# The order of two weight loads at the seam of a scan-and-routing kernel, and the place of four sums

## Chip, cores and metric

One core of a Trainium2 chip. The metric is the device time of one execution in microseconds (us). The kernel before was run three times; one further execution was profiled. PE is TensorE (PEld its weight loads), DVE is VectorE, ACT is ScalarE, POOL is GpSimd, and SP is the queue of SyncE, from which most DMAs are issued.

## What is computed

An attention block (a chunked state-space scan) gives one row of 256 numbers for each of 3072 tokens. Then each token goes through one of eight experts, chosen by its id; the order of the tokens is that of the batch and the sequence.

```python
# scan, per chunk c of 32 steps (batch 4, 8 heads, 768 steps, head dim 32, state dim 16)
y_intra = einsum('bhij,bhjd->bhid', CB * L, xc)
y_inter = einsum('bhin,bhnd->bhid', Cc, state) * decay_to_i
state   = decay_full * state + sum_j(B_j x_j decay_from_j)
# bridge: (B,H,S,D) -> (B*S, H*D) = (3072, 256)
expert_idx = token_ids * 2654435761 % 8
for e in range(8):
    xe = x[expert_idx == e]
    out[expert_idx == e] = maximum(xe @ w1[e], 0) @ w2[e]     # 256 -> 1024 -> 256
```

## The kernel before, in words

**Two parts.** The scan runs first, in six pairs of 64 steps; its rows y are stored to the DRAM tensor `y_tokens` (L407). A routing table is computed meanwhile. The second part goes over the experts in an order of falling token counts; the p-th expert in that order is called place p (`regs[p]` holds its number). Its tokens are taken from `y_tokens` by indirect DMAs on POOL (`gather`, L628, one tile of 128 tokens each), transposed on PE (`turn`, L636, or `early`, L648) and copied out of PSUM into `xT` (by DVE at L654, by ACT at L642).

**Seven products for eight.** Each product of an expert is cut in two by two blocks and done as seven block products with sums of operands in the manner of Strassen and Winograd. `sums_w(p, 1, j, eng)` (L782) makes the four weight sums of place p's first weights, from `w` into `s`; `sums_w(p, 2, j, eng)` those of the second weights; `sums_x` (L882) the four sums of a place's tokens, in `t1`; `sums_h` (L891 to L898) those of its hidden rows, in `t2`. The sums of one set are used in the order 2, 1, 3, 0 of their slices. `up(p, q0, what)` (L917) does block product `what` for two of the four row blocks of the hidden layer; 1 and 2 need weights as loaded, of the first half only, and the early token slots; 3, 5, 6 and 7 need the weight sums, 4 the second half of the weights. The products 6, 7 and 4 add onto one PSUM bank, which DVE reads in between (u2, L932; u3, L935; hx, L941), and 5 and 3 onto another (L944, L939). `down(p, what)` (L964) does the same for the second product.

**Loads.** `load_w1(p, i)` (L616) loads half i of place p's first weights, 512 KB; `load_w2(p)` (L620) the second weights, 1024 KB. All are issued by SP, in program order: an instruction of SP that waits holds up all behind it.

**The seam.** The token slots are laid out so that the first halves of places 0 to 3 (tiles 0 to 6, called EK) come from the first 16 of 24 blocks of steps and can be gathered early. Place 3's early slots are 600 to 792, tiles 4, 5 and 6. Tiles 7 and 8 (`need(0)`) hold place 0's second half; they are gathered when the last store of y has landed. A loop over `seq`, m = 0 to 15, does products 1 and 2 of places 0 to 3 on the early slots. Into it are put: the transposes of tiles 2 to 6 (m = 2, 6, 10), DVE's weight sums of places 0, 1 and 2 (m = 5, 8 and 11), the transposes of the two late tiles (m = 13, 14) and DVE's token sums of place 0 (m = 15). m = 12 to 15 are place 3's products. Right behind m = 0, SP gets a DMA of one number from the last late tile into `held` (L1051), which makes SP wait until that tile has landed, and then three loads.

**The steps.** `step(p)` does, interleaved over its rounds r, the remaining up-products of place p and the down-products of place p - 1, the transposes and gathers of later places, POOL's weight sums (`sums_w(p, 2, ...)` and, from step 1 on, `sums_w(p + 2, 1, ...)`) and DVE's token and hidden sums. Step 0 has five rounds, with the up-products 6, 7, 5, 4, 3. The order of each engine's instructions is the order of the program.

```python
    for w in ((1, 1), (2, 1), (3, 0)):                       # L1025
        load_w1(*w)
...
        if m == 8:                                           # L1038
            for j in range(4):
                sums_w(1, 1, j, dve)
        if m == 11:
            for j in range(4):
                sums_w(2, 1, j, dve)
...
        if m == 0:                                           # L1050
            sp_e.dma_start(out=held[:], in_=xg[need(0)[-1]][0:1, 0:1])
            for w in (0, (3, 1), 1):
                load_w2(w) if isinstance(w, int) else load_w1(*w)
```

Of the kernel before, what the change touches and what calls it, by code (L numbers as in the profile page):

```python
# [25 lines left out]
def kernel(  # L26
# [12 lines left out]
    dve, act, pe, pool_e, sp_e = nc.vector, nc.scalar, nc.tensor, nc.gpsimd, nc.sync  # L39
# [7 lines left out]
    E, _, F = moe_w1.shape  # L47
# [564 lines left out]
    def load_w1(p, i, eng=sp_e):  # L612
        if p not in w1s:
            w1s[p] = (w4[0] if p % 4 == 3 else wpool).tile([P, DP, F], F32, name="w1")
        src = moe_w1[bass.ds(regs[p], 1), :, i * FH:(i + 1) * FH].rearrange("e (k p) f -> p (e k) f", p=P)
        eng.dma_start(out=w1s[p][:, :, i * FH:(i + 1) * FH], in_=src)  # L616

    def load_w2(p, eng=sp_e):
        w2s[p] = wx[0].tile([P, FP, DM], F32, name="w2", bufs=2)
        eng.dma_start(out=w2s[p], in_=moe_w2[bass.ds(regs[p], 1)].rearrange("e (k p) d -> p (e k) d", p=P))  # L620
# [139 lines left out]
    def early(m):  # L760
        turn_pair([q for q in EK if q // 2 == m], (3, 2, 7, 6)[m], dve)
# [3 lines left out]
    def sums_w(p, layer, i, eng):  # L765

        if layer == 1:
            w = w1s[p]
            q = lambda i, k: w[:, k, i * FH:(i + 1) * FH]
            if p not in s1:  # L770
                s1[p] = (spool if p % 3 else s1pool).tile([P, 4, FH], F32, name="s1")
            s = s1[p]
        else:
            w = w2s[p]
            q = lambda i, k: w[:, k * Q4:(k + 1) * Q4, i * P:(i + 1) * P]
            if p not in s2:
                s2[p] = spool.tile([P, 4, Q4, P], F32, name="s2")
            s = s2[p]
        i = (2, 1, 3, 0)[i]
        a_, b_, o = ((q(1, 0), q(1, 1), OP.add), (s[:, 2], q(1, 1), OP.add), (q(1, 0), q(0, 0), OP.subtract),  # L780
                     (q(0, 1), s[:, 1], OP.subtract))[i]
        eng.tensor_tensor(out=s[:, i], in0=a_, in1=b_, op=o)  # L782
        if eng is pool_e and i in (0, 3):
            eng.tensor_copy(out=space, in_=s[:, i, 0, 0:1] if layer == 2 else s[:, i, 0:1])
# [90 lines left out]
    def sums_x(p, i):  # L875
        n = HALF[p]
        q = lambda k, j: xT[:, k, slots(p, j)]
        if i == 0:
            t1[p] = mwork.tile([P, 4, N0], F32, name="t1")
        t = t1[p][:, :, 0:n]  # L880
        a_, b_ = ((q(0, 1), q(0, 0)), (q(1, 1), t[:, 0]), (q(0, 1), q(1, 1)), (q(1, 0), t[:, 1]))[i]
        dve.tensor_tensor(out=t[:, i], in0=a_, in1=b_, op=OP.subtract)  # L882

    def sums_h(p, i):
        n = HALF[p]
        if i == 0:
            t2[p] = hpool.tile([P, 4, Q4, N0], F32, name="t2", bufs=1)
        t = t2[p][:, :, :, 0:n]
        q = lambda k, j: hx[p][:, {(0, 1): 0, (1, 0): 1, (1, 1): 2}[k, j], :, 0:n]
        if i == 0:  # L890
            dve.scalar_tensor_tensor(out=t[:, 0], in0=q(0, 1), scalar=0.0, in1=h11[p][:, :, 0:n],  # L891
                                     op0=OP.max, op1=OP.subtract)
        elif i == 1:
            dve.tensor_tensor(out=t[:, 1], in0=q(1, 1), in1=t[:, 0], op=OP.subtract)
        elif i == 2:
            dve.scalar_tensor_tensor(out=t[:, 2], in0=q(0, 1), scalar=0.0, in1=q(1, 1), op0=OP.max, op1=OP.subtract)  # L896
        else:
            dve.tensor_tensor(out=t[:, 3], in0=q(1, 0), in1=t[:, 1], op=OP.subtract)  # L898
# [100 lines left out]
    def scatter(o_sb, idx):  # L999
        st = pool_e.indirect_dma_start(  # L1000
            out=out[:], out_offset=bass.IndirectOffsetOnAxis(ap=idx, axis=0),
            in_=o_sb, in_offset=None, bounds_check=NT - 1, oob_is_err=False)
        tc.declare_no_dep(st.ins, group="out_rows", reason="distinct rows")
        tc.add_to_no_dep_group("out_rows", st.ins)
# [12 lines left out]
    def turn(k):  # L1017
        if k not in turned:
            turn_x(k, XB)
            turned.add(k)  # L1020
# [1 line left out]
    need = lambda p: [k for k in tiles_of(p) if k not in EK] if p < E else []  # L1022
    outs = sorted(range(NK), key=lambda k: (done_at[k], k))

    for w in ((1, 1), (2, 1), (3, 0)):  # L1025
        load_w1(*w)
    ask(need(0))
    first = [(p, q0) for p in range(NEAR) for q0 in (0, 2)]
# [3 lines left out]
    for m, (what, i) in enumerate(seq):  # L1032
        if m in (2, 6, 10):
            early((m + 2) // 4)
        if m == 5:
            for j in range(2, 4):
                sums_w(0, 1, j, dve)
        if m == 8:  # L1038
            for j in range(4):
                sums_w(1, 1, j, dve)  # L1040
        if m == 11:
            for j in range(4):
                sums_w(2, 1, j, dve)
        if m in (13, 14):
            turn(need(0)[m - 13])
        if m == 15:
            for j in range(4):
                sums_x(0, j)
        up(*first[i], what, banks=(i % 6,) * 2)
        if m == 0:  # L1050
            sp_e.dma_start(out=held[:], in_=xg[need(0)[-1]][0:1, 0:1])  # L1051
            for w in (0, (3, 1), 1):
                load_w2(w) if isinstance(w, int) else load_w1(*w)

    UP = [1, 6, 2, 7, 5, 4, 3]
    UP_E = [6, 7, 5, 4, 3]
    DOWN = [1, 2, 6, 5, 7, 4, 3]

    def step(p):

        ups = [] if p == E else UP_E if p < NEAR else UP
        downs = DOWN if p > 0 else []
        turns = [k for k in need(p + 1) if k not in turned]
        puts = [k for k in outs if done_at[k] == p - 2]
        gets = [k for w in ((2,), (3, 4))[p] for k in need(w) if k not in asked] if p < 2 else need(p + 3)
        sums = [(p, 2, i) for i in range(4)] if p < E else []
        sums += [(p + 2, 1, i) for i in range(4)] if 0 < p < E - 2 else []
        xs_ = [(p + 1, i) for i in range(4)] if p + 1 < E else []
        R = 5 if p == 0 else 7
        off = 0 if p == 0 else (R - len(ups)) // 2  # L1070
        sent = []
        for r in range(R):
            if p > 0 and (r == 0 or p >= NEAR and r < 4):
                sums_h(p - 1, r)
            if sent:
                scatter(*sent.pop(0))
            if gets and p == 0:
                ask(gets)
                gets = []
            if 0 <= r - off < len(ups):  # L1080
                up(p, 0, ups[r - off])
            if turns:
                turn(turns.pop(0))
            if puts:
                sent.append(put(puts.pop(0)))
            if sums and not (p == 1 and r < 4):
                sums_w(*sums.pop(0), pool_e)
            if gets and r >= 1:
                ask([gets.pop(0)])
            if 0 <= r - off < len(ups):  # L1090
                up(p, 2, ups[r - off])
            if 0 < p < NEAR and 0 < r < 4:
                sums_h(p - 1, r)
            if sums and r == 3 and p != 1:
                sums_w(*sums.pop(0), pool_e)
            if p >= NEAR and r >= 3 and not turns and xs_:
                sums_x(*xs_.pop(0))
            if p == 1 and r == 4:
                pool_e.tensor_copy(out=space, in_=t2[0][:, 3, 0, 0:1])
            if p == E - 1 and r == R - 1:  # L1100
                sums_h(p, 0)
            if downs:
                down(p - 1, downs[r])
                if downs[r] == 4 and p + 1 < E:
                    load_w2(p + 1)
            if p < NEAR and r >= (2 if p == 0 else 3) and not turns and xs_:
                sums_x(*xs_.pop(0))
        while xs_ or turns:
            if turns:
                turn(turns.pop(0))  # L1110
            else:
                sums_x(*xs_.pop(0))
        for o in sent:
            scatter(*o)
        for v in sums:
            sums_w(*v, pool_e)
        if p + 4 < E:
            load_w1(p + 4, 0)
            load_w1(p + 4, 1)
        for k in gets:  # L1120
            ask([k])

    for p in range(E):
        step(p)
# [48 lines left out]
    for m in range(2):  # L1173
        scatter(o_own[m], idx_out[:, rest[m]:rest[m] + 1])

    _, rn = nc.values_load_multi_w_load_instructions(
        nov_i[0:1, 0:1], min_val=0, max_val=NCH + E,
        skip_runtime_bounds_check_because="a count of tiles: at most one an expert besides the full ones")
    kf = route.tile([P, 1], F32)
    dve.memset(kf, float(NK))  # L1180
    with tc.For_i(0, rn[0], 1):
# [9 lines left out]
        for c in range(NCH):  # L1191
# [14 lines left out]
        _, re = nc.values_load_multi_w_load_instructions(  # L1206
            ei_i[0:1, 0:1], engines=[ET.SP], min_val=0, max_val=E - 1,
            skip_runtime_bounds_check_because="an expert's number, clamped to E - 1")
# [52 lines left out]
```

## Time and profile before

| | |
|---|---|
| three runs | 231.1, 235.72, 237.67 us (median 235.72) |
| the profiled execution | 231.41 us, its span 229.7 us |
| PE busy | 213.5 us, 93% of the span |
| DVE busy | 180.7 us, 79% |
| POOL busy | 172.4 us, 75% |
| ACT busy | 89.4 us, 39% |
| mean granted TensorE clock | 0.992 of full speed |

A busy share is an average over stages with different limits. Matmuls are pipelined, so that a busy PE is an engine with work in it. Times in rows count from the first instruction of the execution. In a row of the timeline the bracket at the end gives the idle time of that engine just before the instruction, and what ended it.

### The profile page before, as it was taken

What the parts mean: (1) busy time and instruction counts of PE and PEld (TensorE: products, weight loads), DVE (VectorE), ACT (ScalarE), POOL (GpSimd) and SP (SyncE); (2) the same over time, 40 slices, a digit from 0 to 9 for tenths busy, and PEclk for the clock granted to TensorE, in tenths of its full rate; (3) what the DMA queues carried; (4) which work ended last, traced back from release to release, by engine and by line L of the source; (5) the groups of instructions that cost most, each with busy time, mean ns of one, the idle gap of its engine ahead of it and who ended that gap; (6) DMA issues with size and microseconds to landing.
All of it is one profiled execution on the core that took longest, in us unless ns stands there. A gap on an engine that the chain in (4) does not pass through costs nothing.

```text
span 229.7 us, 5853 instructions
## 1 busy us (share of the span) xinstructions
PE 213.5 (93%) x2266; PEld 200.5 (87%) x2266; DVE 180.7 (79%) x314; ACT 89.4 (39%) x190; POOL 172.4 (75%) x220
## 2 busy tenths in 40 slices
PE   6889989998786899999999999999999999999990
PEld 2778878877685799999999999999999999999980
DVE  7868899798547688899997998697489979956630
ACT  4774965954443551312123214234323411413210
POOL 7977367866717198489988998999799999996342
PEclk9999999999999999999999999999999999999996
DMA  6999799999888885029019119307005112401011
GB/s 136 162 200 127 181 191 177 174 185 302 273 218 259 253 267 199 24 75 332 30 62 334 64 47 339 118 7 244 26 24 204 33 45 79 175 23 47 24 70 43
DMA packets 49877, 33.16 MB, mean 144 GB/s; under 512 B 26632, under 2 KB 44184, under 8 KB 49850
## 3 DMA queue, kind: packets, MB, share of 16 engines
q1 hardware_dynamic: 46786, 25.76, 45.6%
q0 software_dynamic: 2400, 6.43, 8.5%
q10 hardware_dynamic: 664, 0.61, 1.1%
q8 instruction: 18, 0.29, 0.5%
q14 instruction: 9, 0.07, 0.1%
HBM read 26.49 MB, written 6.42 MB: 143 GB/s over the span
## 4 chain that ended last, share of the span: by engine, by line
PE 73%; DMA 8%; DVE 7%; ACT 6%; issue 2%; SPq 1%; POOL 1%; ACTq 0%; DVEq 0%; POOLq 0%
PE ps L964 31%; PE ps L917 28%; PE ps L315 4%; DMA w<-in_moe_w_dram 3%; DMA xg<-y_tokens,idx_in 3%; PE ps L991 2%; PE ps L374 2%; PE ps L636 2%; DMA y_tokens<-y_sb 2%; DVE m L321 1%; ACT z L358 1%; PE ps L387 1%; PE ps L269 1%; DVE rows L259 1%; ACT ct L289 1%
## 5 line engine op out<-in xcount | busy, mean ns | idle before, releaser
L628 POOL DMA_INDIRECT xg<-y_tokens,idx_in x25 | 30.2, 1206 | 17.1 <-issue 10.1
L917 PE MATMUL ps<-t,s 128*128 128x202 f32 (+7 forms) x192 | 37.1, 328 | 0.6 <-DVE t L882 0.6
L782 POOL TENSOR_TENSOR s<-w 128x512 f32<-128x512 f32 x26 | 33.2, 1277 | 5.7 <-DMA w<-in_moe_w_dram 5.5
L1000 POOL DMA_INDIRECT out_dram<-o_sb,idx_out x25 | 26.4, 1056 | 12.5 <-ACT o_sb L996 6.7
L964 PE MATMUL ps<-t,s 128*128 128x202 f32 (+7 forms) x192 | 35.5, 326 | 0.0
L917 PEld LDWEIGHTS ps<-t,s 128*128 128x128 f32 x192 | 31.5, 190 | 1.3 <-ACT h L927 0.9
L964 PEld LDWEIGHTS ps<-t,s 128*128 128x128 f32 x192 | 31.8, 189 | 0.3 <-issue 0.3
L917 PE MATMUL ps<-xT,w 128*128 128x200 f32 (+7 forms) x128 | 24.9, 329 | 3.0 <-DMA w<-in_moe_w_dram 2.3
L917 PEld LDWEIGHTS ps<-xT,w 128*128 128x128 f32 x128 | 20.7, 190 | 3.8 <-DVE s L782 2.5
L945 ACT ACTIVATE hx<-hx 128x404 f32<-128x404 f32 (+7 forms) x16 | 8.3, 525 | 31.8 <-DVE hx L944 31.3
L321 DVE COPY_PREDICATED m<-cmask,ps 128x1024 f32<-128x1024 int32 x12 | 15.5, 1320 | 3.6 <-PE ps L315 3.6
L782 POOL TENSOR_TENSOR s<-w,s 128x512 f32<-128x512 f32 x13 | 17.6, 1351 | 0.5
L782 POOL TENSOR_TENSOR s<-s,w 128x512 f32<-128x512 f32 x13 | 17.3, 1327 | 0.5
L882 DVE TENSOR_TENSOR t<-xT 128x202 f32<-128x202 f32 (+7 forms) x16 | 16.4, 1024 | 0.8 <-ACT xT L642 0.8
L923 ACT ACTIVATE p<-ps 128x404 f32<-128x404 f32 (+7 forms) x16 | 7.9, 492 | 20.0 <-PE ps L917 19.7
L374 PEld LDWEIGHTS ps<-x_t,m 128*64 128x64 f32 x384 | 12.1, 138 | 3.0 <-issue 1.3
L374 PE MATMUL ps<-x_t,m 128*64 128x64 f32 x384 | 13.4, 224 | 1.1 <-ACT y_sb L401 0.6
L315 PE MATMUL ps<-ce,bt 32*64 32x128 f32 x384 | 12.9, 274 | 1.1 <-ACT ce L289 0.7
L882 DVE TENSOR_TENSOR t<-xT,t 128x202 f32<-128x202 f32 (+7 forms) x16 | 13.7, 854 | 0.0
L896 DVE SCALAR_TENSOR_TENSOR t<-hx 128x808 f32<-128x808 f32 (+7 forms) x8 | 13.3, 1660 | 0.0
L315 PEld LDWEIGHTS ps<-ce,bt 32*64 32x64 f32 x384 | 10.4, 132 | 2.5 <-ACT ce L289 0.9
L358 ACT ACTIVATE z<-z,half 128x256 f32<-128x256 f32 x22 | 10.0, 504 | 6.6 <-DVE z L352 6.6
(201 smaller groups left out, 472.5 us busy)
## 6 DMA issues: line engine op xcount, KB each, us to landing
w<-in_moe_w_dram SPq DMA_DIRECT2D x16, 512.0 KB, 7.1
w<-in_moe_w_dram SPq DMA_DIRECT2D x8, 1024.0 KB, 8.0
x_t<-in_x_dram SPq DMA_DIRECT2D x12, 256.0 KB, 6.2
y_tokens<-y_sb SPq DMA_DIRECT2D x10, 256.0 KB, 4.3
raw<-in_B_dram SPq DMA_DIRECT2D x12, 128.0 KB, 3.5
raw<-in_C_dram SPq DMA_DIRECT2D x12, 128.0 KB, 3.5
y_tokens<-y_sb ACTq DMA_DIRECT2D x2, 256.0 KB
xg<-y_tokens,idx_in POOLq DMA_INDIRECT x25, 3.5
```

What stands on the lines that cost most here:

```text
L315: pe.matmul(out=ps[u * T:(u + 1) * T, GB + g, b * P:(b + 1) * P].rearrange("q (e i) -> q e i", e=2), lhsT=bts[ck][r, b, c], rhs=ces[ck][r, ...
L321: dve.copy_predicated(out=m_sb[k % 2][:, g0:g1].rearrange("q g b i -> q g (b i)"), mask=cmask.bitcast(I32).rearrange("q j i -> q (j i)").u ...
L358: act.activation(z4s[un][:, :, j], zs[un].rearrange("q b e d -> q b (e d)"), AF.Copy, scale=half4[:, j:j + 1])
L374: pe.matmul(out=o, lhsT=m_sb[k % 2][:, g, b, e * T:(e + 1) * T], rhs=xs[k][:, b, 2 * g + e], start=first(g // 2 * 2 + b % 2, c), stop=True ...
L628: pool_e.indirect_dma_start(out=xg[k], out_offset=None, in_=y_dram[0:n, :], in_offset=bass.IndirectOffsetOnAxis(ap=idx_in[:, k:k + 1], axi ...
L782: eng.tensor_tensor(out=s[:, i], in0=a_, in1=b_, op=o)
L882: dve.tensor_tensor(out=t[:, i], in0=a_, in1=b_, op=OP.subtract)
L896: dve.scalar_tensor_tensor(out=t[:, 2], in0=q(0, 1), scalar=0.0, in1=q(1, 1), op0=OP.max, op1=OP.subtract)
L917: pe.matmul(out=ps[:, bank, i * n:(i + 1) * n], lhsT=lhs[:, (q0 + i) * P:(q0 + i + 1) * P], rhs=rhs, start=(first and i == 0), stop=True, ...
L945: act.activation(hq(2), hq(2), AF.Relu)
L964: pe.matmul(out=ps[:, bank, 0:n], lhsT=lhs(q), rhs=rhs(q), start=(first and q == 0), stop=True, skip_group_check=True)
L1000: st = pool_e.indirect_dma_start(out=out[:], out_offset=bass.IndirectOffsetOnAxis(ap=idx, axis=0), in_=o_sb, in_offset=None, bounds_check= ...
```

## The change

Of the three loads ahead of the seam's loop, (2,1) is taken out and put first behind the `held` DMA. The loads ahead of the loop are now (1,1), (3,0); behind `held` come (2,1), the second weights of place 0, (3,1), and the second weights of place 1. The four DVE sums of place 2's first weights leave m = 11 and go into step 0, one in each of the rounds 0 to 3, behind the round's second up-product.

```diff
-    for w in ((1, 1), (2, 1), (3, 0)):
+    for w in ((1, 1), (3, 0)):
         load_w1(*w)
...
-        if m == 11:
-            for j in range(4):
-                sums_w(2, 1, j, dve)
...
         if m == 0:
             sp_e.dma_start(out=held[:], in_=xg[need(0)[-1]][0:1, 0:1])
-            for w in (0, (3, 1), 1):
+            for w in ((2, 1), 0, (3, 1), 1):
                 load_w2(w) if isinstance(w, int) else load_w1(*w)
 
+    late_sums = [0, 1, 2, 3]
...
             if p == E - 1 and r == R - 1:
                 sums_h(p, 0)
+            if p == 0:
+                for _ in range((1, 1, 1, 1, 0)[r]):
+                    sums_w(2, 1, late_sums.pop(0), dve)
             if downs:
                 down(p - 1, downs[r])
```

## Rows read from the trace of the kernel before

**Rows 1.** The page's first line: the span and its instructions.
```profile
span 229.7 us, 5853 instructions
```
**Rows 2.** Busy by stretch: length, PE, PEld, DVE, ACT, POOL (instructions); clock; DMA; GB/s.
```profile
72.00:74.00 2.00, 0.18 (x1) 0.21 (x2) 1.97 (x5) 0.09 (x1) 1.39 (x3) 1.00 0.62 217
78.00:214.00 136.00, 136.00 (x854) 134.84 (x855) 114.63 (x173) 39.82 (x97) 115.29 (x111) 1.00 0.37 125
```
**Rows 3.** Timeline of PE, seam to step 1: start, duration, line, operation, tiles, count.
```profile
73.82 0.89 PE L917 MATMUL ps<-xT,w 128*128 128x192 f32 x4 [2.27 <-DMA w<-in_moe_w_dram]
...
77.89 0.95 PE L917 MATMUL ps<-t,s 128*128 128x202 f32 x4 [0.58 <-DVE t L882]
...
86.96 1.51 PE L917 MATMUL ps<-t,s 128*128 128x200 f32 x8
...
89.69 1.52 PE L917 MATMUL ps<-t,s 128*128 128x200 f32 x8
91.04 1.53 PE L964 MATMUL ps<-t,s 128*128 128x202 f32 x8
```
**Rows 4.** From the chain that ended last, 44 to 92 us: load (3,0), issue to landing.
```profile
66.55 7.14 DMA w<-in_moe_w_dram
```
**Rows 5.** Timeline of the SP queue at the seam: issues of weight loads and `held`.
```profile
64.82 2.10 SPq L616 DMA_DIRECT2D w<-in_moe_w_dram  x3
74.43 0.32 SPq L1051 DMA_DIRECT2D held<-xg  x1
75.00 0.40 SPq L620 DMA_DIRECT2D w<-in_moe_w_dram  x1
```
**Rows 6.** Landing times of load (1,1), then of the gathers of tiles 7 and 10.
```profile
DMA to landing us min/median/max: 5.1/5.1/5.1
...
DMA to landing us min/median/max: 5.8/5.8/5.8
...
DMA to landing us min/median/max: 2.8/2.8/2.8
```
**Rows 7.** Timeline of DVE: first sum of place 1, tile 6, first sum of place 2.
```profile
69.97 0.69 DVE L782 TENSOR_TENSOR s<-w 128x512 f32<-128x512 f32 x1 [1.98 <-DMA w<-in_moe_w_dram]
...
72.64 0.42 DVE L654 COPY xT<-ps 128x256 f32<-128x256 f32 x1
72.97 0.68 DVE L782 TENSOR_TENSOR s<-w 128x512 f32<-128x512 f32 x1
```
**Rows 8.** Timeline of POOL: the gather of tile 8, the first sum of w2(0).
```profile
69.56 1.00 POOL L628 DMA_INDIRECT xg<-y_tokens,idx_in  x1 [0.30 <-PE ps L917]
...
80.71 1.27 POOL L782 TENSOR_TENSOR s<-w 128x512 f32<-128x512 f32 x1 [5.46 <-DMA w<-in_moe_w_dram]
```
**Rows 9.** Timeline of DVE in step 0 and the start of step 1.
```profile
79.78 0.58 DVE L932 TENSOR_TENSOR u<-ps,p 128x404 f32<-128x404 f32 x1 [0.26 <-PE ps L917]
...
81.47 0.58 DVE L935 TENSOR_TENSOR u<-ps,p 128x404 f32<-128x404 f32 x1 [0.33 <-PE ps L917]
...
84.70 0.36 DVE L882 TENSOR_TENSOR t<-xT,t 128x200 f32<-128x200 f32 x1
...
86.77 0.99 DVE L891 SCALAR_TENSOR_TENSOR t<-hx,h 128x808 f32<-128x808 f32 x1
87.84 1.25 DVE L932 TENSOR_TENSOR u<-ps,p 128x400 f32<-128x400 f32 x2
89.01 1.00 DVE L894 TENSOR_TENSOR t<-hx,t 128x808 f32<-128x808 f32 x1
...
91.73 0.99 DVE L896 SCALAR_TENSOR_TENSOR t<-hx 128x808 f32<-128x808 f32 x1
```
**Rows 10.** Timelines of POOL and DVE in step 2, where two instructions collide.
```profile
104.32 1.28 POOL L782 TENSOR_TENSOR s<-s,w 128x512 f32<-128x512 f32 x1
105.68 1.91 POOL L782 TENSOR_TENSOR s<-w,s 128x512 f32<-128x512 f32 x1
...
104.39 2.07 DVE L891 SCALAR_TENSOR_TENSOR t<-hx,h 128x800 f32<-128x800 f32 x1
```

## The prediction

> **What bounds the kernel now.** I read the page first, then the busy time by stretch, then the instructions of TensorE (PE), VectorE (DVE), GpSimd (POOL) and the SP queue around the seam, and last the landings there. The span is 229.7 us [rows 1]. From 78 to 214 us PE is busy for all 136.00 of 136.00 us, while DVE and POOL are busy for some 115 each [rows 2]: in the routed part PE sets the end, so a stall of PE that is taken away before 78 us shortens the kernel one for one, and any new stall lengthens it one for one. The stretch 72 to 74 us is the hole the change aims at: PE works 0.18 of 2.00 us there [rows 2].
>
> In that hole PE waits 2.27 us, until 73.82, for the first half of place 3's first weights, load (3,0) [rows 3]. That load is issued at 66.55 and lands 7.14 later, at 73.69 [rows 4]. It stands third behind (1,1) and (2,1), all issued by SP from 64.82 on [rows 5]. (1,1) lands 5.1 after its issue, at 69.92 [rows 6]; so two half loads (and gathers between them) take 73.69 - 69.92 = 3.77 us, 1.9 each.
>
> But a second thing is due at nearly the same time. The matmuls at 73.82 belong to `up(3,0,1)`, whose slots 600 to 792 need token tile 6 too. DVE's copy of that tile out of PSUM ends at 72.64 + 0.42 = 73.06, because it stands in DVE's program order behind the four sums of place 1, which begin only when (1,1) has landed, at 69.97 [rows 7]. So behind the DMA wait lies a DVE wait that ends 0.63 us sooner.
>
> **The change, part by part.**
>
> (a) *(3,0) asked for before (2,1).* It takes the second place in the queue, so it should land one half load earlier, near 73.69 - 1.9 = 71.8. Then the copy at 73.06 is late next. With the same 0.13 us from landing to matmul as now, PE resumes at 73.19 in place of 73.82: a gain of 0.63. Bounds: 0 if (3,0) lands no earlier, 2.27 if the copy came early enough as well. I take 0.6, since the copy's chain starts from (1,1), whose place in the queue is not changed. Everything between 73.82 and `up(0,0,6)` at 77.89 (transposes, evictions, the sums of place 0's tokens) follows in its present 4.07 us, so that step 0 starts at about 77.3.
>
> (b) *(2,1) behind the held DMA.* The held DMA, which waits for token tile 8, goes out at 74.43 and the next load at 75.00 [rows 5]. Tile 7's gather took 5.8 us beside the weights, tile 10's, after them, 2.8 [rows 6]. Tile 8's is issued at 69.56 [rows 8], so with a half load less in its way it lands between 69.56 + 2.8 = 72.4 and the present 74.4; I take 72.7. (2,1) is then issued at 73.3 and, by (1,1)'s 5.1, lands at 78.4. What now queues behind it on SP are the second weights of place 0, the other half of place 3's and the second weights of place 1. POOL's first sum of w2(0) starts at 80.71 now [rows 8]; it moves by -1.7 (the wait) and +1.9 (one half load more), to 80.9. PE's first use of such a sum is the `down(0,6)` at 91.04 [rows 3], and the second sum is done some 2.7 us after POOL's start: over 7 us of room cover it. Without that cover it would cost the 0.2.
>
> (c) *Four DVE sums moved into step 0.* In before they run from 72.97 on [rows 7], where PE waits for data and DVE has nothing that is late: taking them out gives nothing. In step 0 they come one each after the second `up` of r = 0 to 3, at 0.69 us each [rows 7], 2.76 in all. DVE there is full: between the end of the second u2 at 80.36 and the first `sums_h` at 86.77 [rows 9] its longest idle time is the 0.33 before the second u3.
>
> First who waits for DVE. `up(1,0,6)` at 86.96 reads the second token sum, which is done at 84.70 + 0.36 = 85.06: 1.9 us of room. (A reader waits for the slice it reads, not for the tile: `down(0,6)` starts at 91.04 [rows 3] while the third `sums_h`, which writes another slice of the same tile and stands earlier in the program, ends at 91.73 + 0.99 = 92.72 [rows 9].) `up(1,0,7)` at 89.69 [rows 3] adds onto the bank that the first u2 has to read, done at about 88.47: 1.2 us of room. `down(0,6)` at 91.04 needs the second `sums_h`, done at 89.01 + 1.00 = 90.01 [rows 9]: 1.0 of room.
>
> *Low end, sums at their 0.69.* On the clock of before (PE unmoved): S0 80.36 to 81.05, both u3 to 82.2, S1 to 82.9, the rest pushed by 0.74, then 1.43 with S2, 2.1 with S3. The second token sum is done at 87.25: PE waits 0.3. The first u2 is read at 90.6: 0.7 more. The second `sums_h` ends at 92.3: 0.3 more. In all 1.3 us.
>
> *High end, sums that collide with POOL.* POOL's sums of w2(0), 1.27 us each [rows 8], run through this very stretch. How a DVE instruction with two operands in SBUF fares beside one is shown 20 us later: the `sums_h` of 104.39 takes 2.07 us, though 0.99 is its length elsewhere [rows 9], and it ends 0.86 after POOL's instruction (104.32 + 1.28 = 105.60); POOL's next one, at 105.68, takes 1.91 for the same reason, the other way round [rows 10]. The DVE instructions that read PSUM keep their 0.58. I walk it with whole turns: POOL starts at 81.5 on this clock. S0 is clear. S1 begins at 82.2, waits for POOL's first sum and ends at 83.3. Then POOL's second runs to 84.5, S2 begins at 84.4 and ends at 85.1. POOL's third runs to 86.4 and the first token sum waits for it, to 86.65. S3 begins at 87.7, waits for POOL's fourth (86.9 to 88.2), ends at 88.8. The second token sum is done at 89.15, against 85.06 now: `up(1,0,6)` goes at 89.2, 2.25 late. The first u2 is read at 92.4: 0.5 more. The second `sums_h` ends at 93.9: 0.2 more. In all 2.9 us.
>
> I take 2.9, since the collision is nearest to rows 10: same kinds of instruction, same engines. By the sums' own row alone, 0.69 beside POOL's gathers, it would be the 1.3.
>
> The Trainium skill, page "SBUF — State Buffer", section "SBUF: two separate sides", puts it as an exclusive lock: a VectorE instruction with two SBUF inputs and a GpSimd instruction that reads SBUF exclude each other for the whole instruction, and the loser fully blocks. Rows 10 agree (2.07 for 0.99). No row of before shows these very sums against POOL's; by the rule the sum would be +2.3, by the sums' own row +0.7, so this rule speaks against the change.
>
> **Sum:** -0.6 + 2.9 = +2.3 us, on a profiled execution of 231.41 (its span 229.7). The three timed runs are 231.1, 235.72 and 237.67, so that execution is near the fastest; I set the sum against the mean of these four, 233.98, and forecast 236.3 us. Against the median alone it would be 238.0.
>
> **The rivals.**
> 1. *No collision.* POOL's sums of w2(0) come later, or DVE slips between them. For it: the gap between POOL's sums; against it: rows 10. -0.6 + 1.3 = +0.7: 234.7.
> 2. *Shorter than before.* (1,1) lands earlier, having fewer loads beside it; the copy of tile 6 then comes earlier too and the whole 2.27 is gained. -2.27 + 1.3 = -1.0: 233.0. It decides from the point where (1,1) lands 0.7 us earlier and the sums don't collide. For it: the second load is in flight before (1,1) has landed [rows 5, 6]. Against it: (1,1) keeps its place at the head of the three.
> 3. *(2,1) late.* S0 waits for it, and behind S0 on DVE stand the u3, for which PE's `up` 4 waits. S0 is due at 80.36 - 0.6 = 79.8; each us past it adds one. Slower by 2% (4.7 us) is reached if (2,1) lands at 82.2, 8.9 after its issue. Half loads landed after 5.1 and 7.14 [rows 4, 6]; the held DMA at its present time alone gives 80.1, or +0.3. Price: some 5 us, 239.
> 4. *The change does not do what it says.* (3,0) lands no earlier, the gathers taking the freed time; the sums still cost 2.9: 236.9.
>
> **How the numbers follow.** Chances: forecast 0.38, rival 1 0.22, rival 2 0.20, rival 3 0.08, rival 4 0.12. The forecast's own range is the fastest and slowest run shown plus 2.3: 233.4 to 240.0. The whole range goes from the fastest run with rival 1's +0.7, 231.8, to the slowest with rival 4's +2.9, 240.6; left out are rival 2 on a fast run and the far part of rival 3, together under 0.2. About 2% is what a measurement of this kernel can tell from no change. Over 2% slower: most of rival 3 and the runs' spread on top of the forecast, 0.12. Over 2% faster: rival 2 with that spread, 0.03. Within: 0.85.
>
> **What would show it.** Right: PE's wait for weights near 72 us gone, its matmuls of `up(3,0,1)` starting just behind DVE's copy of tile 6 near 73.1; step 0 starting near 77.3; DVE's moved sums at 0.69 to 1.3 us with POOL's sums between them; a new wait of PE for DVE before `up(1,0,6)` of some 2 us. Wrong: that wait absent or under 0.5 (then rival 1 or 2), PE at `up(3,0,1)` before 72.5 (rival 2), or DVE waiting for weights before its first moved sum (rival 3).

## The result and the profile after

Over 22 executions of each kernel, taken side by side, the changed kernel took 1.0115 times the time of the kernel before, 95% interval 1.0078 to 1.0152: on the 235 us of before that is +2.7 us, between 1.8 and 3.6. The forecast was +2.3. The ratio leaves out executions more than 1.5% above the fastest of their kernel, whereas the medians of all 22 are 235.62 us after and 235.1 before, only 0.5 apart, so that the size is less sure than the interval says. In a later comparison, on a chip where both kernels took some 240 us, the ratio was 1.004 (0.9996 to 1.0083).

The profiled execution of after has a longer span, but most of that is none of the change's doing. The page's first line, then PE's timeline from the last early tokens to step 1 (start, duration, line, operation, tiles, count; in brackets the idle time before, and what ended it), with one row of PE's weight loads and the first of the closing transposes:

```profile
span 235.0 us, 5851 instructions
```
```profile
62.86 0.44 PE L648 MATMUL ps<-ident,xg 128*128 128x128 f32 x2 [2.55 <-DMA xg<-y_tokens,idx_in]
64.27 3.06 PE L917 MATMUL ps<-xT,w 128*128 128x202 f32 x8
...
75.22 2.47 PE L917 MATMUL ps<-xT,w 128*128 128x198 f32 x12
...
76.77 0.62 PEld L917 LDWEIGHTS ps<-xT,w 128*128 128x128 f32 x4 [0.32 <-DVE xT L654]
...
80.87 0.95 PE L917 MATMUL ps<-t,s 128*128 128x202 f32 x4 [0.58 <-DVE t L882]
...
91.63 1.62 PE L917 MATMUL ps<-t,s 128*128 128x200 f32 x8 [1.42 <-DVE t L882]
...
94.55 1.62 PE L917 MATMUL ps<-t,s 128*128 128x200 f32 x8
96.31 1.61 PE L964 MATMUL ps<-t,s 128*128 128x202 f32 x8
97.75 1.52 PE L917 MATMUL ps<-t,s 128*128 128x200 f32 x8
...
227.33 0.38 PE L1138 MATMUL ps<-ident,xT 128*128 128x128 f32 x2
```

Three things are to be seen. The hole at `up(3,0,1)` is nearly gone: its matmuls are the last four of the twelve that begin at 75.22 (the bracket of [rows 3] had 2.27 us). What is left is the 0.32 us that their weight loads stand idle, for DVE's copy of tile 6. A new wait stands further on: 1.42 us before `up(1,0,6)` at 91.63, for DVE. And the execution was already late when it came to the seam: the matmuls of place 2 behind the transposes of tile 6 start at 75.22, against 70.02 in before, because PE waited 2.55 us for an early gather and eight matmuls behind it took 3.06 us at a lower clock (last section). Those instructions precede everything that was changed.

So I compare distances that start behind such lateness. A is from those matmuls of place 2 to step 0 (`up(0,0,6)`); it holds the hole, though it still depends on how far the loads have come by then. B is from there to `up(1,0,5)` in step 1; it holds what steps 0 and 1 pay. C is from there to the closing transposes (L1137, L1138 in after). The other ends of A, B and C in before (77.89 is in [rows 3]):

```profile
70.02 1.53 PE L917 MATMUL ps<-xT,w 128*128 128x198 f32 x8
...
92.41 1.51 PE L917 MATMUL ps<-t,s 128*128 128x200 f32 x8
...
222.00 0.38 PE L1137 MATMUL ps<-ident,xT 128*128 128x128 f32 x2
```

In before A = 7.87, B = 14.52 and C = 129.59. In after A = 80.87 - 75.22 = 5.65, nearly the whole hole less, B = 97.75 - 80.87 = 16.88, that is 2.36 more (the wait above, and its successors), and C = 129.58: nothing further on has changed. In these two traces gain and cost nearly cancel; A varies from execution to execution, as the experiments show.

The longer stretch of [rows 2], 78 to 214 us, now holds 2.1 us in which PE is idle: the 1.42 before `up(1,0,6)`, and the 0.58 before step 0, which before has too (at 77.89, ahead of that stretch).

```profile
78.00:214.00 136.00, 133.86 (x834) 131.15 (x833) 115.65 (x174) 40.76 (x101) 113.82 (x108) 1.00 0.40 131
```

DVE's timeline shows the chain of the seam and the four moved sums (L782 from 83.26 on); POOL's, its sums of w2(0) beside them:

```profile
73.64 0.69 DVE L782 TENSOR_TENSOR s<-w 128x512 f32<-128x512 f32 x1 [0.43 <-DMA w<-in_moe_w_dram]
...
76.30 0.42 DVE L654 COPY xT<-ps 128x256 f32<-128x256 f32 x1
...
83.26 0.68 DVE L782 TENSOR_TENSOR s<-w 128x512 f32<-128x512 f32 x1
...
84.95 1.49 DVE L782 TENSOR_TENSOR s<-s,w 128x512 f32<-128x512 f32 x1
...
87.34 0.79 DVE L782 TENSOR_TENSOR s<-w,s 128x512 f32<-128x512 f32 x1
88.05 1.43 DVE L882 TENSOR_TENSOR t<-xT 128x200 f32<-128x200 f32 x1
...
90.37 0.93 DVE L782 TENSOR_TENSOR s<-w 128x512 f32<-128x512 f32 x1
91.22 0.36 DVE L882 TENSOR_TENSOR t<-xT,t 128x200 f32<-128x200 f32 x1
```
```profile
72.25 1.00 POOL L628 DMA_INDIRECT xg<-y_tokens,idx_in  x1 [0.30 <-PE ps L648]
...
84.62 1.27 POOL L782 TENSOR_TENSOR s<-w 128x512 f32<-128x512 f32 x1 [7.37 <-DMA w<-in_moe_w_dram]
85.97 1.60 POOL L782 TENSOR_TENSOR s<-s,w 128x512 f32<-128x512 f32 x1
87.65 1.60 POOL L782 TENSOR_TENSOR s<-w,s 128x512 f32<-128x512 f32 x1
```

The second moved sum starts at 84.95 inside POOL's instruction of 84.62, ends 0.55 after it and so takes 1.49 for 0.68. POOL's next, 85.97, takes 1.60 in turn. The first token sum (88.05) takes 1.43 for 0.36 beside POOL's 87.65. The second token sum ends at 91.22 + 0.36 = 91.58, and PE goes at 91.63.

The SP queue at the seam:

```profile
67.44 1.79 SPq L616 DMA_DIRECT2D w<-in_moe_w_dram  x2
75.59 0.32 SPq L1048 DMA_DIRECT2D held<-xg  x1
```

Tile 8, issued at 72.25, lets `held` go 3.34 us later (4.87 before, from [rows 8] and [rows 5]).

### The profile page after: what moved, and what is told of

Its sections match the earlier page's. It is cut to its first block, busy times and chain, and to the rows that moved or that the text cites. A ratio compares the mean times of both kernels' runs of the same rounds, so it can differ in the third digit from the quotient of the medians.

```text
span 235.0 us, 5851 instructions
## 1 busy us (share of the span) xinstructions
PE 217.2 (92%) x2266; PEld 202.1 (86%) x2266; DVE 183.0 (78%) x314; ACT 89.3 (38%) x190; POOL 172.7 (73%) x220
## 4 chain that ended last, share of the span: by engine, by line
PE 72%; DVE 14%; ACT 4%; issue 4%; DMA 3%; POOL 2%; DVEq 0%; POOLq 0%; ACTq 0%
PE ps L964 30%; PE ps L917 28%; DVE m L321 4%; DMA xg<-y_tokens,idx_in 3%; PE ps L315 3%; PE ps L991 2%; PE ps L159 2%; DVE t L882 1%; PE ps L636 1%; PE ps L374 1%; PE ps L269 1%; DVE z L352 1%; POOL rows L259 1%; DVE s L782 1%; PE ps L1166 1%
## 5 line engine op out<-in xcount | busy, mean ns | idle before, releaser
L628 POOL DMA_INDIRECT xg<-y_tokens,idx_in x25 | 29.6, 1182 | 19.7 <-DVE wfa L595 7.0
L782 POOL TENSOR_TENSOR s<-w 128x512 f32<-128x512 f32 x26 | 33.2, 1277 | 7.7 <-DMA w<-in_moe_w_dram 7.4
L917 PE MATMUL ps<-xT,w 128*128 128x200 f32 (+7 forms) x128 | 26.4, 342 | 0.8 <-DVE xT L654 0.8
L917 PEld LDWEIGHTS ps<-xT,w 128*128 128x128 f32 x128 | 21.9, 198 | 1.6 <-DVE xT L654 1.5
L945 ACT ACTIVATE hx<-hx 128x404 f32<-128x404 f32 (+7 forms) x16 | 8.3, 525 | 33.4 <-DVE hx L944 33.0
L882 DVE TENSOR_TENSOR t<-xT 128x202 f32<-128x202 f32 (+7 forms) x16 | 17.3, 1080 | 2.8 <-ACT xT L642 2.8
L782 POOL TENSOR_TENSOR s<-w,s 128x512 f32<-128x512 f32 x13 | 17.8, 1365 | 0.5
L782 POOL TENSOR_TENSOR s<-s,w 128x512 f32<-128x512 f32 x13 | 17.6, 1352 | 0.5
L942 ACT ACTIVATE hx<-hx 128x404 f32<-128x404 f32 (+7 forms) x16 | 8.2, 526 | 12.3 <-DVE hx L941 11.9
```

Of the source, the lines that this page charges most:

```text
L628: pool_e.indirect_dma_start(out=xg[k], out_offset=None, in_=y_dram[0:n, :], in_offset=bass.IndirectOffsetOnAxis(ap=idx_in[:, k:k + 1], axi ...
L917: pe.matmul(out=ps[:, bank, i * n:(i + 1) * n], lhsT=lhs[:, (q0 + i) * P:(q0 + i + 1) * P], rhs=rhs, start=(first and i == 0), stop=True, ...
L942: act.activation(hq(1), hq(1), AF.Relu)
L945: act.activation(hq(2), hq(2), AF.Relu)
```

## The experiments

Theory A is the prediction's: at the seam two things gate `up(3,0,1)`, load (3,0) and DVE's copy of tile 6 behind place 1's sums, so that the new order of the loads gives only what lies between them; the moved sums collide with POOL's and cost 1.3 to 2.9 us. Its rivals are named in the expectations. Each ratio is to the kernel before on the same chip; 0.1% is about 0.24 us. A, B and C are the distances above; C is 129.6 where it isn't given. The edits of the first two groups are against the changed kernel except f1's, which is against before; those of the last group are told of one by one.

### The changed kernel again, and its two halves

> The changed kernel once more, beside the others. Theory A (collisions): +2.3 us against the kernel before: the seam gives 0.6 (up to 2.27 where the copy of tile 6 is early enough), the four DVE sums in step 0, blocked by POOL's sums, take 2.3 to 2.9 back as waits of PE for DVE before up(1,0,6), up(1,0,7) and down(0,6). Rival B (late weights): the first moved sum waits for load (2,1). Rival C (nothing freed): PE still waits at up(3,0,1).

Ratio 1.004 (0.9996 to 1.0083): +1.0 us, not clear of none. A is 9.60 in its trace and B 15.64. The hole is back, with the copy of tile 6 named as its end (PE, then DVE):

```profile
79.92 0.92 PE L917 MATMUL ps<-xT,w 128*128 128x192 f32 x4 [2.49 <-DVE xT L654]
...
82.18 2.73 PE L917 MATMUL ps<-xT,w 128*128 128x192 f32 x8
```
```profile
79.45 0.42 DVE L654 COPY xT<-ps 128x256 f32<-128x256 f32 x1
```

The copy ends at 79.87 and PE starts at 79.92. Here DVE's first sum of place 1, for which (1,1) is the last thing to come, starts 76.78 - 70.21 = 6.57 us after the first issue of the weights (5.15 in before), so DVE's four sums and the copy behind them came late, and it made no difference where (3,0) stood. (The eight matmuls of 82.18 are told of at the end.)

> Only the loads in their new order; the four sums of place 2's first weights are left out (their tile is filled with zeros at m = 11), so this does less DVE work than either kernel. Theory A: only the gain of the seam is left, -0.6 us, and up to -2.3 if the copy of tile 6 is not the gate; no wait of PE for DVE before up(1,0,6), which stands 9.07 us behind up(0,0,6) as before. Rival C: 0. If the reordered loads themselves cost something later (second weights of place 0 later), the time is above before.

```diff
         if m == 11:
+            s1[2] = spool.tile([P, 4, FH], F32, name="s1")
+            dve.memset(s1[2], 0.0)
...
-            if p == 0:
-                for _ in range((1, 1, 1, 1, 0)[r]):
-                    sums_w(2, 1, late_sums.pop(0), dve)
```

Ratio 0.9994 (0.9945 to 1.0042): -0.1 us, between -1.3 and +1.0. B is 14.53, before's 14.52: without the sums steps 0 and 1 pay nothing. A is 7.63, and the copy is again what PE waited for:

```profile
80.74 0.92 PE L917 MATMUL ps<-xT,w 128*128 128x192 f32 x4 [2.01 <-DVE xT L654]
```

The loads alone gave nothing that these runs can tell. C is 129.93.

> Only the four sums moved into step 0; the loads in their old order. Theory A: the hole at m = 12 is as before (2.27 us), and the sums cost their full 2.3 to 2.9 us: +2.3 to +2.9, with up(1,0,6) some 10.8 us behind up(0,0,6) in place of 9.07. Rival B (the cost is (2,1) landing late): here (2,1) has landed long before, so +0 to +0.5.

```diff
-    for w in ((1, 1), (3, 0)):
+    for w in ((1, 1), (2, 1), (3, 0)):
...
-            for w in ((2, 1), 0, (3, 1), 1):
+            for w in (0, (3, 1), 1):
```

Ratio 1.0094 (1.0045 to 1.0143): +2.3 us. The sums alone cost what the theory said, with (2,1) landed long before; rival B is out. B is 16.09, 1.57 more than before. A is 8.19; here too the copy (79.27 + 0.42 = 79.69) and PE's start meet:

```profile
79.74 0.92 PE L917 MATMUL ps<-xT,w 128*128 128x192 f32 x4 [2.56 <-DVE s L782]
```
```profile
79.27 0.42 DVE L654 COPY xT<-ps 128x256 f32<-128x256 f32 x1
```

So with the old order of loads, too, the copy was the last gate on this chip.

> The changed kernel with POOL's four sums of place 0's second weights left out (their tile is filled with zeros by DVE at m = 11, where DVE is idle), so that the moved DVE sums have nothing to collide with in step 0. Theory A: the sums take 0.69 us each, none is stretched; the cost in steps 0 and 1 falls from 2.3 to the low end, 1.3 or less: +0.7 against before in place of +2.3. Rival D (DVE is simply too full, collisions don't matter): the cost stays at 2.3.

```diff
         if m == 11:
+            s2[0] = spool.tile([P, 4, Q4, P], F32, name="s2")
+            dve.memset(s2[0], 0.0)
...
-        sums = [(p, 2, i) for i in range(4)] if p < E else []
+        sums = [(p, 2, i) for i in range(4)] if 0 < p < E else []
```

Ratio 0.9958 (0.9905 to 1.0012): -1.0 us, where +0.7 was expected; 2.0 less than the changed kernel beside it. B is 15.12, 0.60 above before. All four moved sums take 0.68 or 0.69, and the first token sum its own length:

```profile
89.98 0.68 DVE L782 TENSOR_TENSOR s<-s,w 128x512 f32<-128x512 f32 x1
...
92.15 0.36 DVE L882 TENSOR_TENSOR t<-xT 128x200 f32<-128x200 f32 x1
...
95.25 1.17 DVE L882 TENSOR_TENSOR t<-xT 128x200 f32<-128x200 f32 x1
```
```profile
94.92 1.27 POOL L782 TENSOR_TENSOR s<-w 128x512 f32<-128x512 f32 x1 [11.47 <-DMA w<-in_moe_w_dram]
```

The same instructions took 1.49 and 1.43 in after. Rival D falls: with nothing of POOL's beside the four sums themselves B is only 0.60 above before, and `up(1,0,6)` stands 94.98 - 85.93 = 9.05 behind step 0, as early as in before (9.07). Part of the 0.60 is a collision again: the third token sum (95.25) takes 1.17 for some 0.36 beside POOL's first remaining sum, and PE then waits 0.32 us at `up(1,0,7)`. The rest of after's 2.36 is collision.

### The gate of the copy

> The kernel before with one edit: place 1's four sums go from m = 8 to m = 11, so that DVE's copy of tile 6 no longer stands behind them and load (1,1). Theory A (the copy gates up(3,0,1) about as late as the load does): PE then waits only for load (3,0), which is third in the queue: 0 to -0.8 us. Rival E (only the load gates it): no change at all, and the hole keeps its length to 0.1 us.

```diff
-        if m == 8:
+        if m == 11:
             for j in range(4):
                 sums_w(1, 1, j, dve)
```

Ratio 0.9982 (0.9926 to 1.0038): -0.4 us, not clear of none. A is 7.12 and B 14.95. The end of the hole changed hands, as theory A has it (PE, then the first issue of the weights on SP):

```profile
82.66 0.89 PE L917 MATMUL ps<-xT,w 128*128 128x192 f32 x4 [1.52 <-DMA w<-in_moe_w_dram]
```
```profile
72.55 2.37 SPq L616 DMA_DIRECT2D w<-in_moe_w_dram  x3
```

> The changed kernel with the same edit. Theory A: both gates are gone, up(3,0,1) starts right behind the matmuls before it or on (3,0)'s landing in second place; the hole shrinks from some 2.5 us to under 1; step 0 starts 1.5 to 2.5 us earlier in relation to place 2's products than in the changed kernel, unless the transposes of tiles 7 and 8 are late next; the sums in step 0 still cost 1 to 2.4: between -1.0 and +0.5 against the kernel before. Rival E: no change against the changed kernel.

The same edit on the changed kernel. Ratio 0.9963 (0.9916 to 1.0011). A is 6.50, and only 0.90 us of the hole is left, for the load; but B is 16.63, and C is 130.14, with a wait of 0.51 us for DVE at 113.30:

```profile
77.48 0.89 PE L917 MATMUL ps<-xT,w 128*128 128x192 f32 x4 [0.90 <-DMA w<-in_moe_w_dram]
...
92.22 1.62 PE L917 MATMUL ps<-t,s 128*128 128x200 f32 x8 [1.44 <-DVE t L882]
```
```profile
69.68 1.75 SPq L616 DMA_DIRECT2D w<-in_moe_w_dram  x2
```

Rival E falls: on this chip the hole is 0.90 us with both gates moved (0.94 in f9), 1.08 with the loads alone (f8, where PE's row names the copy) and 1.52 with the copy alone (f1). The margin to f8 is small.

> The changed kernel with the copy of tile 6 first, again, on the chip of the other two. From the run before: -0.9 us against the kernel before, between -2.0 and +0.3; its step 0 pays 1.6 to 2.1 us, which f4_third_load does not, so it should be longer than that one by 0.5 to 1.5.

Ratio 1.0027 (0.9975 to 1.0079): +0.6 us, outside the expected -2.0 to +0.3. A is 7.00, B 16.07, C again 130.14. The two comparisons of this kernel differ by 0.64%: what the seam gives back and the steps take is about equal by these ratios.

### Other places for the four sums

> The changed kernel with the four late sums on POOL, in step 0 ahead of its sums of the second weights, where POOL waits 5 to 8 us for load w2(0). Theory A: DVE's extra work in step 0 is gone, up(1,0,6) stands about 9.1 us behind up(0,0,6) as in the kernel before; POOL's sums of w2(0) end some 2 us later, which their 7 us of room cover; only the seam's gain is left, which on a chip where the copy of tile 6 gates is 0 to -0.6. Rival: POOL becomes late for down(0,6) or down(0,5), +1 or more.

```diff
             if gets and p == 0:
                 ask(gets)
                 gets = []
+                for j in late_sums:
+                    sums_w(2, 1, j, pool_e)
...
-            if p == 0:
-                for _ in range((1, 1, 1, 1, 0)[r]):
-                    sums_w(2, 1, late_sums.pop(0), dve)
```

(Against the changed kernel.) Ratio 1.0026 (0.9982 to 1.0071): +0.6, no gain. A is 6.70 and B 14.81, nearly before's; but POOL's sums of w2(0) now run on to 100, into step 1, beside DVE's hidden sums, and PE waits further on, twice, where neither before nor after has a wait. C is 132.13, 2.5 more than theirs. POOL, then PE:

```profile
88.02 1.27 POOL L782 TENSOR_TENSOR s<-w 128x512 f32<-128x512 f32 x1 [4.62 <-DMA w<-in_moe_w_dram]
...
97.93 2.04 POOL L782 TENSOR_TENSOR s<-w 128x512 f32<-128x512 f32 x1
```
```profile
118.08 1.61 PE L917 MATMUL ps<-t,s 128*128 128x198 f32 x8 [1.03 <-DVE u L932]
...
203.22 1.54 PE L964 MATMUL ps<-t,w 128*128 128x188 f32 x8 [1.20 <-DVE du L981]
...
234.55 0.38 PE L1137 MATMUL ps<-ident,xT 128*128 128x128 f32 x2
```

That these two waits come from the sums on POOL is borne out by the next run, which has both; the chain between them and step 0 is not followed here. The prediction's "over 7 us of room" of POOL is room towards `down(0,6)` only; it is no room towards DVE. The first row also times (2,1), which was issued at 82.90: 5.1 us.

> Both: late sums on POOL and the copy of tile 6 first. Theory A: the whole hole at m = 12 goes and nothing is paid in step 0: -1.5 to -2.5 us against the kernel before. Rival (tokens): the transposes of tiles 7 and 8, or their copies on ACT, are late next and leave -0.5.

(Both edits, against the changed kernel.) Ratio 1.0036 (0.9996 to 1.0075): +0.9, where -1.5 to -2.5 was expected. A is 6.54, but B is 16.50 and C 132.10, with waits of 1.00 us at 115.02 and 1.20 at 200.16 for the same instructions of DVE as in f8_sums_on_pool (f2_after_copy_first, which differs from this run in the place of the sums alone, has only its 0.51 at 113.30). The first collision has moved to the hidden sums, which the u2 behind them and so `up(1,0,7)` pay for:

```profile
96.22 1.62 PE L917 MATMUL ps<-t,s 128*128 128x200 f32 x8 [1.36 <-DVE u L932]
```
```profile
93.61 2.06 DVE L891 SCALAR_TENSOR_TENSOR t<-hx,h 128x808 f32<-128x808 f32 x1
```

Theory A expected the whole hole to go, but 0.94 us of it is left, and it gave a longer POOL no price.

> The kernel before with (3,0) and (2,1) exchanged in the queue, nothing put behind the held DMA, and the sums of places 1 and 2 both at m = 11, behind the copy of tile 6. Theory A: the hole at m = 12 shrinks as in f2_after_copy_first (to 1 us or less, on (3,0) in second place), and nothing is paid in step 0, where up(1,0,6) stands 9.1 us behind up(0,0,6): -1.0 to -2.0 us. Rival (late sums): DVE's sums of place 2 now wait for (2,1) in third place, 2 us later than before, and push the token sums at m = 15, so that step 0 starts no earlier: 0.

```diff
-    for w in ((1, 1), (2, 1), (3, 0)):
+    for w in ((1, 1), (3, 0), (2, 1)):
...
-        if m == 8:
+        if m == 11:
             for j in range(4):
                 sums_w(1, 1, j, dve)
```

(Against before.) Ratio 1.0002 (0.9962 to 1.0041), where -1.0 to -2.0 us was expected, though its trace has the shortest A + B with the sums in the work: 6.77 + 14.49 (before: 7.87 + 14.52). The wait at `up(3,0,1)` is gone, and two others stand in its place, for a late token tile and, as its rival had it, for the token sums that stand behind the sums of (2,1):

```profile
82.18 0.44 PE L636 MATMUL ps<-ident,xg 128*128 128x128 f32 x2 [0.69 <-DMA xg<-y_tokens,idx_in]
...
85.98 0.92 PE L917 MATMUL ps<-t,s 128*128 128x202 f32 x4 [1.15 <-DVE t L882]
```

> As f4_third_load, but the last of place 2's four sums goes into round 0 of step 0. Theory A: one sum of 0.69 us there falls into the room that up(1,0,7) and down(0,6) have (1.0 to 1.2 us), so it costs under 0.3, and the token sums start 0.7 earlier: equal to f4_third_load or up to 0.5 shorter. If one sum already costs 0.7 or more, DVE has no room at all in step 0.

```diff
-            for j in range(4):
+            for j in range(3):
                 sums_w(2, 1, j, dve)
...
+            if p == 0 and r == 0:
+                sums_w(2, 1, 3, dve)
             if downs:
                 down(p - 1, downs[r])
```

(Against f4_third_load.) Ratio 0.990 (0.9851 to 0.9948): -2.4 us. A is 7.54 and B 14.49: one sum in round 0 costs nothing up to there. C is 129.84.

> f5_one_late once more, to see whether its gain holds: 0.990 of the kernel before in the first comparison. If the gain is that of the seam (hole at m = 12 shortened, step 0 paying under 0.3 us), it should come out between 0.985 and 0.998; a ratio of 1 or more would mean that the first comparison was luck of the runs.

Ratio 0.9949 (0.9869 to 1.0029) on another chip, inside what was expected but not clear of 1. A is 7.34, B 14.50. Its step 0 has no wait at `up(1,0,6)` (PE; then DVE's one moved sum, which is over before POOL's first begins):

```profile
80.58 0.92 PE L917 MATMUL ps<-t,s 128*128 128x202 f32 x4 [0.84 <-DVE t L882]
...
89.63 1.51 PE L917 MATMUL ps<-t,s 128*128 128x200 f32 x8
```
```profile
82.94 0.68 DVE L782 TENSOR_TENSOR s<-w 128x512 f32<-128x512 f32 x1
```
```profile
84.12 1.27 POOL L782 TENSOR_TENSOR s<-w 128x512 f32<-128x512 f32 x1 [7.34 <-DMA w<-in_moe_w_dram]
```

It came out below the kernel before both times; its traces explain only 0.1 and 0.6 us of that (A + B 22.03 and 21.84, against 22.39, and 0.25 back in the first one's C). Whether it is better than f4_third_load stays open: on their chip the ratios put it 1% below, the medians of all executions 0.5 us above (238.09 against 237.62).

## Why the prediction was right, point by point

*The sum and its sign.* +2.3 was forecast, +2.7 (1.8 to 3.6) measured, then +1.0 on the second chip. The forecast, "seam gives little, step 0 takes more", is the one that held. That the total came so near is in part luck: by the runs the seam gives 0.1 (e1) where 0.6 was forecast, and the sums cost 2.3 (e2) where 2.9 was, and the two errors cancel.

*(a) The seam, -0.6.* The mechanism held: behind the load stands the copy of tile 6. After_again, e1 and e2 show it as PE's last gate, and f1 and f2 hand the wait back to the load by moving the copy alone. The size is no constant. In after's own trace nearly the whole 2.27 went, because PE came to the seam 5.2 us later than before while (1,1) landed only 3.7 later (73.64 against 69.97), so that the copy was done at 76.72, and PE's matmuls of `up(3,0,1)` could start at 76.77; in after_again nothing went. The runs give -0.1 (-1.3 to +1.0) for the loads alone. The forecast's 0.6 was one execution's difference of two arrivals that are not coupled. That execution was the odd one: DVE's first sum of place 1 starts 5.15 us after the first issue of the weights in it (69.97 - 64.82), and 6.06 to 6.57 in the six other traces whose row names that load. The new order of the loads isn't shown to be the reason: e2, with the old one, stands at 6.31, though its row names no load.

*(b) Loads behind `held`.* Tile 8 was forecast to land 3.1 us after its issue (72.7 - 69.56) and let `held` go after 3.34; (2,1) was given 5.1 and took 5.1 (f8). The first moved sum didn't wait for it in any trace: rival 3 is out. POOL's start was put 3.6 behind step 0 and came 3.75 behind (84.62 - 80.87).

*(c) The sums, +2.9.* B rose by 2.36 in after, 1.57 in e2, 1.12 in after_again. The waits stood where they were forecast: before `up(1,0,6)`, 1.69 us late against the 2.25 of the walk, then at `up(1,0,7)` and `down(0,6)`, in all 2.29 late where 2.9 was forecast (`down(0,6)` at 96.31 - 80.87 = 15.44 behind step 0, against 13.15). The waits on POOL were sized about right in sum: the walk has 0.4 + 0 + 1.2 + 0.4 = 2.0 us of them (second and third sum, first token sum, fourth sum), the trace 0.81 + 0.11 + 1.07 + 0.25 = 2.24 (1.49, 0.79 and 0.93 less 0.68, and 1.43 less 0.36), with nearly all of it on one sum and the token sum. What was mis-sized is how the instructions follow on each other. The second token sum was walked to end 11.26 us behind step 0 (89.15 - 77.89) and ended after 10.71 (91.58 - 80.87), 0.55 sooner in spite of the 0.24 more of waiting. The walk laid the records end to end; in the trace each begins some 0.08 us before the record of the one ahead of it ends (91.22 against 90.37 + 0.93 = 91.30), 0.72 over the nine from the second u2 to the second token sum. [rows 9] show it in before, too (89.01 against 87.84 + 1.25 = 89.09).

B is not one number for the same sums, and POOL's start behind step 0 differs with it: 3.75 us in after (B 16.88), 2.58 in e2 (16.09), 2.04 in after_again (15.64). But 4.93 in f2_repeat goes with 16.07 and 5.49 in f2 with 16.63, so that the start alone does not set the cost. The choice between the ends of the range was right: e3 took POOL's sums away and left 0.60. The low end, 1.3, was therefore itself too large. The rule of the Trainium skill that was weighed there (page "SBUF — State Buffer", section "SBUF: two separate sides", the exclusive lock between a VectorE instruction with two SBUF inputs and a GpSimd instruction that reads SBUF) held for these sums: 1.49 beside POOL's, 0.68 without.

*Rival 1* (no collision, +0.7) is refuted by after's rows. *Rival 4* has (3,0) land no earlier. With the copy out of the way, PE starts `up(3,0,1)` 82.66 - 72.55 = 10.11 us after the first issue of the weights where (3,0) is third (f1), and 9.00 in before, third too; where it is second, 7.80 (f2: 77.48 - 69.68), 8.32 (f2_repeat), 7.82 (f9), 8.46 and 8.44 (the two of f5). f1, f2 and f9 ran on one chip. All five are sooner than both others, so (3,0) does land earlier, by 0.5 us at least, and rival 4 is out; its total, +2.9, lies inside the measured interval, so that the total alone would not have told it from the forecast. *Rival 2* has the right A in one execution (nearly the whole hole gone) but by another cause: (1,1) landed not sooner but later after its issue (6.20 us against 5.15), and it was PE that came late. Its total was wrong, since the sums did collide.

*What stays open.* The two traces of before and after differ by only 22.53 - 22.39 = 0.14 us in A + B, while the executions differ by 2.7 by the ratio. One trace is one draw of A, which ranged from 5.65 to 9.60 in the same kernel; the runs, not the trace, carry the size. And comparisons of one kernel differed by 0.5 to 0.75% from chip to chip (after 1.0115 and 1.004, f2 0.9963 and 1.0027, f5 0.990 and 0.9949), more than I can account for from the traces. The medians of all executions agree better: after 0.5 and 0.4 us above the kernel before (235.62 and 235.1; 240.55 and 240.14), f2 1.1 and 1.5 below it (239.13 and 240.24; 238.36 and 239.81), f5 1.7 and 1.1 below (238.09 and 239.81; 233.54 and 234.6). By them f4_third_load, with a ratio of 1.0002, is 2.2 below (237.62 and 239.81). Both counts put after above the kernel before; which is nearer to the true size the runs don't settle.

## What to carry to other kernels

Before a load is moved up to close a hole, look for the second thing that becomes due just behind it; here a copy, in program order behind four sums that wait for another load, was done 0.6 us ahead of the first gate in one execution, and was itself the last gate in every other trace that kept it there. Work that is taken out of an engine's idle time and put beside a neighbour with which it collides costs more than it does alone (here at most 0.60 us without POOL's sums, up to 2.36 beside them), and handing it to the neighbour moved PE's waits to later steps rather than ended them. When executions vary by more than the effect, measure distances between instructions inside the trace, and let many runs carry the total.

## What was not expected of the hardware

The granted TensorE clock dropped to about half of full speed, the lower of its two levels (1.2 of 2.4 GHz), for some microseconds after some waits of PE, and not after others. In after_again PE had idled 2.49 us before 79.92; from 82 to 85 us the clock column of the windows (after the busy times) shows 0.55, and eight matmuls took 2.73 us that take 1.47 at full clock (in after, at 78.82). In after it was the stretch behind the 2.55 us that PE waited for an early gather:

```profile
82.00:85.00 3.00, 2.91 (x10) 2.44 (x8) 1.30 (x4) 1.36 (x4) 0.00 (x0) 0.55 0.91 282
```
```profile
64.00:67.00 3.00, 3.00 (x22) 2.82 (x13) 1.92 (x4) 1.10 (x2) 1.92 (x2) 0.54 0.57 195
```

The hole of 2.27 us in before was followed by no such drop, nor were those of 2.56 in e2 and 2.92 in e3 (1.00 in the three microseconds behind each), so the length of the wait alone does not tell. In after_again PE's way from `up(3,0,1)` to step 0 took 85.49 - 79.92 = 5.57 us, against 4.07 in before: the drop cost 1.5, as much as half of what the change was about, and whether it falls into the seam is part of why A varies.
